# An early read of 32 bytes a row from the modulation weights, on Pool's queue, into a tile that nobody reads

## The chip, the cores and the metric

The kernel runs on one core of one Trainium2 chip. The metric is the device time of one execution in microseconds (us). The kernel before took 103.14 us, the median of three runs that went from 102.98 to 103.59.

## What is computed

The kernel is the attention half of a diffusion transformer block. With B = 2, N = 256 and D = 1152, all in bf16:

```python
mod = (_silu(c) @ w_mod).reshape(B, 6, 1, D)
shift_a, scale_a, gate_a, shift_m, scale_m, gate_m = [mod[:, i] for i in range(6)]
h = _layernorm(x, axis=-1) * (1 + scale_a) + shift_a
qkv = h @ wqkv
...
p = _softmax(jnp.einsum('bqd,bkd->bqk', q, k) * D ** (-0.5), axis=-1)
a = jnp.einsum('bqk,bkd->bqd', p, v) @ wo
return x + gate_a * a
```

The inputs are x (2 x 256 x 1152), c (2 x 1152), wqkv (1152 x 3456), wo (1152 x 1152) and w_mod (1152 x 6912). Of w_mod's six column groups three are needed: group 0 is the shift, group 1 the scale, group 2 the gate.

## The kernel before

The 512 rows of x are four tiles of 128 rows; D is nine blocks of 128. Every matrix product goes over these nine blocks. Five engines have lists of their own: PE (matrix products and transposes), DVE and ACT (elementwise work and copies out of the accumulators), POOL (setup, small powers, the gate's sum over partitions) and SP, which issues nearly all loads and stores. PE's, DVE's and ACT's orders are written out by hand: each operation is recorded in a list (all of these have line 75, that of the recording helper), and `pin` at the end chains each list. POOL's and SP's orders are left to a scheduler.

POOL begins with setup (L95 to L110): zeros in `ident` and, with `affine_select` (L97), ones on its diagonal; `ones_bf` (L102), `ones_row` (L104), `junk_rhs` (L106), `eps_t` (L108) and `neg_half` (L110). In the built program ones_bf is written ahead of the diagonal.

SP issues c (L115), two of x's four tiles (L118, ACT issues the other two), then w_mod's scale group in nine slices of 128 rows (L146), the first five 128-column blocks of wqkv (`wA`, L148 to L150), and the nine slices of the shift group (L153). Later come the rest of wqkv (L360), the gate group (L364) and wo (L368). Each transfer that SP or ACT issues takes one of eight completion semaphores in turn, and an issue waits until the transfer eight places before it has landed.

PE transposes c (needs c and ident), runs 13 junk matmuls on junk_rhs (N_JUNK), then starts the scale accumulators with ones_bf and ones_row and adds the nine scale blocks, one per slice, nine small matmuls each, with the transposes of the four normalized x tiles between them. DVE multiplies the transposed tiles by the scale (`hTs`); PE multiplies these by wA, with the nine shift blocks put between the later steps (H_AFTER_K). When the last shift block is done, h itself is formed (`hT`) and the rest runs: q and k, scores, v, softmax, attention, wo, gate.

The change and the steps of the prediction touch L94 to L110 (setup on POOL), L146 (`wm`, scale), L153 (`wm`, shift), the junk matmuls and `scale_block`. w_mod's slice kk is read as 128 rows of 2304 bytes; in the input a row is 13,824 bytes long. The first slice of the scale group is `w_mod[0:128, 1152:2304]`.

Of the kernel before, what the change touches and what calls it, by code (L numbers as in the profile page):

```python
# [11 lines left out]
BF16 = mybir.dt.bfloat16  # L12
# [4 lines left out]
def kernel(  # L17
# [9 lines left out]
    nc = tc.nc  # L27
    P = 128
    B, N, D = x.shape
# [23 lines left out]
    const = ctx.enter_context(tc.tile_pool(name="const", bufs=1))  # L53
# [32 lines left out]
    def pin(seq):  # L86
        names, insts = set(), []
        for r in seq:
            if r.ins.name not in names:
                names.add(r.ins.name)  # L90
                insts.append(r)
        for a, b in zip(insts, insts[1:]):
            tc.add_manual_dep(b.ins, a.ins.name, SCHED, reason="pinned engine order")

    ident = const.tile([P, P], BF16)  # L95
    nc.gpsimd.memset(ident, 0.0)
    nc.gpsimd.affine_select(  # L97
        out=ident, in_=ident, compare_op=ALU.not_equal, fill=1.0, base=0,
        pattern=[[-1, P]], channel_multiplier=1,
    )  # L100
    ones_bf = const.tile([P, P], BF16)
    nc.gpsimd.memset(ones_bf, 1.0)  # L102
    ones_row = const.tile([1, 512], BF16)
# [55 lines left out]
    for jj in range(N_JUNK):  # L159
# [7 lines left out]
        out=scT_f.rearrange("p k b -> p b k"),  # L167
# [117 lines left out]
    for k in range(KT):  # L285
        gi, jj = s_loc(k)
        for b in range(B):
            sl = slice(b * N, (b + 1) * N)
            vec.tensor_scalar(
                out=hTs[:, k, sl], in0=xnT[:, k, sl], scalar1=psS[gi][:, jj, b : b + 1], scalar2=None,  # L290
# [47 lines left out]
    for k in range(KT):  # L338
        for b in range(B):
            sl = slice(b * N, (b + 1) * N)  # L340
            if (2 * k + b) % 3 == 2:
                act_seq.append(sca.activation(
                    out=hT[:, k, sl], in_=xnT[:, k, sl], func=ACT.Identity,
                    bias=sh[:, k, b : b + 1], scale=s1p[:, k, b : b + 1],
                ))
            else:
                dve_seq.append(vec.tensor_scalar(
                    out=hT[:, k, sl], in0=xnT[:, k, sl],
# [23 lines left out]
    for f in range(NACC):  # L372
        for b in range(B):
            sl = slice(b * N, (b + 1) * N)
            if (f * B + b) % 2 == 0:
                dve_seq.append(vec.tensor_scalar(
                    out=qkT[:, f, sl], in0=accs[f][:, sl], scalar1=bias_sb[:, f, b : b + 1],
                    scalar2=None, op0=ALU.add))
            else:
                act_seq.append(sca.activation(  # L380
                    out=qkT[:, f, sl], in_=accs[f][:, sl], func=ACT.Identity,
# [18 lines left out]
    for b in range(B):  # L400
        vec.tensor_scalar(
            out=gacc[:, b, :], in0=wg_k[0], scalar1=scT_f[:, 0, b : b + 1], scalar2=None, op0=ALU.mult
        )
        for kt in range(1, KT):
            vec.scalar_tensor_tensor(
                out=gacc[:, b, :], in0=wg_k[kt],
# [37 lines left out]
    for b in range(B):  # L444
# [7 lines left out]
        for i in range(NQ):  # L452
            sca.activation(
                out=p_f[:, i, :], in_=s_ps[:, i, :], func=ACT.Exp,
# [111 lines left out]
```

## Time and profile before

| What | us |
|---|---|
| median of the runs | 103.14 |
| the profiled execution's span, first to last instruction | 101.7 |
| difference between the two, outside the span | 1.4 |
| PE busy in the span | 93.7 |
| DVE busy | 71.9 |
| ACT busy | 30.4 |
| POOL busy | 28.5 |
| DMA, 16 engines, mean rate over the span | 207 GB/s |
| a packet of 2304 bytes (a row of x or w_mod), median | 0.093 |
| a packet of 128 bytes, median | 0.013 |

The profiled execution's own time is its span; what the median holds beyond it lies before the first and after the last instruction. In the slices, the span is cut into 40 equal parts of 2.54 us, and a digit is the busy share in tenths. In the chain of waits each piece has a start, a length and what the time went to; DMA means that the next step waited for that transfer. In the list of waits the numbers are the total in us, how many times, and the longest. In the table by stretch each engine has its busy time and number of instructions, followed by the granted PE clock, the DMA engines' mean busy share and GB/s. In the list by time the columns are start, length, engine, line, operation, output and inputs, and in brackets how long the engine had been idle and what ended that.

### The profile page before, as it was taken

The page shows a single profiled execution, that of the slowest core. Times are in us where ns is not written, and L with a number is a line of the kernel's source. Part 1 is how long each engine was busy: PE and PEld are TensorE (multiplying, and loading weights), DVE is VectorE, ACT ScalarE, POOL GpSimd, SP SyncE. Part 2 cuts the span into 40 slices and gives each one's busy share as a digit, 9 for nine tenths or more (in the row PEclk, how much of TensorE's full clock was granted, in tenths as well). Part 3 has the DMA queues.
Part 4 walks back from the last instruction along what each step waited for, and adds up shares of the span by engine and source line. Part 5 has one row for each costly group of instructions (what it writes and reads, how often), then busy time and mean ns, then how long its engine had stood idle before and what let it go on. Part 6 is the DMA issues. An engine that isn't in the chain of part 4 may idle for free.

```text
span 101.7 us, 1828 instructions
## 1 busy us (share of the span) xinstructions
PE 93.7 (92%) x723; PEld 55.8 (55%) x729; DVE 71.9 (71%) x129; ACT 30.4 (30%) x61; POOL 28.5 (28%) x28
## 2 busy tenths in 40 slices
PE   0996989997999999999999999999998999999970
PEld 0334974474564444444447866566567856566550
DVE  0999679200899999999999992155226859998760
ACT  5089560000678422422332013551115500000000
POOL 6033300000000000079910000007990039996000
PEclk9999999999999999999999999999999999999999
DMA  2989999999999999999999100000000000202212
GB/s 75 376 304 396 403 391 386 405 395 325 354 374 361 400 377 322 316 327 327 368 406 366 50 0 0 0 0 0 0 0 0 6 0 0 116 0 116 114 54 67
DMA packets 17204, 21.05 MB, mean 207 GB/s; under 512 B 1068, under 2 KB 11692, under 8 KB 17196
## 3 DMA queue, kind: packets, MB, share of 16 engines
q1 hardware_dynamic: 16763, 20.34, 57.3%
q10 hardware_dynamic: 432, 0.61, 1.8%
q8 instruction: 5, 0.08, 0.3%
q14 instruction: 4, 0.02, 0.1%
HBM read 19.76 MB, written 1.18 MB: 206 GB/s over the span
## 4 chain that ended last, share of the span: by engine, by line
PE 71%; DMA 24%; issue 1%; DVE 0%; SPq 0%; ACT 0%
PE ps L75 63%; DMA wm<-in_w_mod_dram 21%; PE s_ps L75 4%; DMA x_sb<-in_x_dram 3%; PE acc_t L75 2%; PE bias_ps L75 1%; DVE pT L75 0%; PE psH L75 0%; SPq L115 0%; PE pT_ps L75 0%; ACT o_sb L75 0%
## 5 line engine op out<-in xcount | busy, mean ns | idle before, releaser
L409 POOL PARTITION_ALL_REDUCE gate_bc<-gacc x2 | 14.1, 7068 | 50.8 <-DVE gacc L75 32.9
L75 DVE SCALAR_TENSOR_TENSOR gacc<-wg_t,scT_f,gacc 128x1152 f32<-128x1152 bf16 x16 | 27.4, 1714 | 0.6
L75 PE MATMUL ps<-hT,wq_t 128*128 128x512 bf16 x114 | 25.3, 379 | 0.2
L75 PEld LDWEIGHTS <-wq_t 128*128 128x128 bf16 x117 | 11.3, 98 | 13.6
L75 PE MATMUL ps<-wq_t,hT 128*128 128x384 bf16 x108 | 17.7, 326 | 0.0
L75 PE MATMUL ps<-wo_t,attnT 128*128 128x384 bf16 x99 | 16.3, 326 | 0.0
L75 PEld LDWEIGHTS <-attnT 128*128 128x128 bf16 x117 | 10.9, 98 | 6.7
L75 PEld LDWEIGHTS <-hT 128*128 128x128 bf16 x108 | 10.6, 98 | 6.9
L75 ACT CAST qkT<-ps 128x512 bf16<-128x512 f32 x13 | 7.6, 585 | 15.4 <-PE ps L75 15.4
L483 POOL TENSOR_TENSOR wo_last<-wo_t,gate_bc 128x384 bf16<-128x384 bf16 x9 | 9.9, 1136 | 7.1 <-issue 7.1
L75 PE MATMUL acc_t<-hTs,wA 128*128 128x512 bf16 x42 | 9.9, 379 | 0.5 <-DVE hTs L75 0.4
L75 DVE TENSOR_TENSOR o_sb<-ga,x_sb 128x384 bf16<-128x384 f32 x11 | 8.1, 736 | 0.4
L75 PEld LDWEIGHTS <-wA 128*128 128x128 bf16 x90 | 5.4, 96 | 5.1 <-issue 0.5
L75 PEld LDWEIGHTS <-wm 128*128 128x128 bf16 x162 | 6.4, 97 | 3.1 <-DMA wm<-in_w_mod_dram 2.3
L75 ACT CAST v_sb<-ps 128x384 bf16<-128x384 f32 x8 | 3.8, 478 | 14.0 <-PE ps L75 14.0
L75 DVE TENSOR_TENSOR ga<-ps,gate_bc 128x384 f32<-128x384 f32 x11 | 6.1, 553 | 2.6 <-PE ps L75 2.5
L75 ACT ACTIVATE hT<-xnT,sh,s1p 128x256 bf16<-128x256 bf16 x6 | 3.1, 588 | 11.7 <-DVE sh L75 11.7
L75 PE MATMUL mps<-scT_rep,wm 128*128 128x96 bf16 x81 | 4.8, 207 | 0.8 <-DMA wm<-in_w_mod_dram 0.7
L75 DVE CAST sh_bf<-psH 128x18 bf16<-128x18 f32 x1 | 0.2, 176 | 7.4 <-PE psH L75 7.4
L75 ACT CAST o_sb<-ps 128x64 bf16<-128x64 f32 x1 | 0.2, 212 | 17.4 <-PE ps L75 17.4
L75 PE MATMUL junk_ps<-junk_rhs,ident 128*128 128x512 bf16 x13 | 4.6, 528 | 0.3 <-POOL neg_half L110 0.3
L75 DVE CAST v_sb<-ps 128x384 bf16<-128x384 f32 x4 | 2.1, 553 | 3.8 <-PE ps L75 3.8
(70 smaller groups left out, 81.3 us busy)
## 6 DMA issues: line engine op xcount, KB each, us to landing
wm<-in_w_mod_dram SPq DMA_DIRECT2D x18, 288.0 KB, 6.6
wq_t<-in_wqkv_dram SPq DMA_DIRECT2D x6, 864.0 KB, 9.7
wg_t<-in_w_mod_dram SPq DMA_DIRECT2D x9, 288.0 KB, 7.1
wo_t<-in_wo_dram SPq DMA_DIRECT2D x9, 288.0 KB, 6.2
wq_t<-in_wqkv_dram SPq DMA_DIRECT2D x2, 576.0 KB, 9.2
out_dram<-o_sb SPq DMA_DIRECT2D x3, 288.0 KB, 2.1
wA<-in_wqkv_dram SPq DMA_DIRECT2D x1, 800.0 KB
x_sb<-in_x_dram ACTq DMA_DIRECT2D x2, 288.0 KB, 3.5
```

Source lines behind the costliest of these rows:

```text
L75: r = fn(*a, **k)
L409: ar = nc.gpsimd.partition_all_reduce(gate_bc[:, b, :], gacc[:, b, :], P, bass.bass_isa.ReduceOp.add)
L483: nc.gpsimd.tensor_tensor(out=wo_last[:, k, :], in0=wo_k[k][:, D - TAILW :], in1=gate_bc[:, B - 1, D - TAILW :], op=ALU.mult)
```

## The change

After the diagonal is written, a tile of 128 rows by 16 columns (32 bytes a row) is read from the first 128 rows of w_mod, from column 1152 on, on POOL's queue. These are the first 32 bytes of each row of the first scale slice. A pin holds the transfer behind the `affine_select`. No instruction reads the tile.

```diff
-    nc.gpsimd.affine_select(
+    sel = nc.gpsimd.affine_select(
         out=ident, in_=ident, compare_op=ALU.not_equal, fill=1.0, base=0,
         pattern=[[-1, P]], channel_multiplier=1,
     )
+    touch = const.tile([P, 16], BF16)
+    touch_dma = nc.gpsimd.dma_start(out=touch, in_=w_mod[0:P, D : D + 16])
+    pin([sel, touch_dma])
```

In the built program POOL's order is then ident, ones_bf, the diagonal, the new transfer, ones_row, junk_rhs, eps_t, neg_half, and the rest as before. The order on PE, DVE, ACT and SP, and the semaphores that SP's and ACT's transfers take, are the same as before.

## Prediction

> **What bounds the kernel now.** I read the slices first, then the chain that ended last, then the waits up to 28 us, then the stretch from 1 to 10 us by microsecond and as a list. The slices give PE, DMA and the bytes moved:
>
> ```profile
> PE   0996989997999999999999999999998999999970
> DMA  2989999999999999999999100000000000202212
> GB/s 75 376 304 396 403 391 386 405 395 325 354 374 361 400 377 322 316 327 327 368 406 366 50 0 0 0 0 0 0 0 0 6 0 0 116 0 116 114 54 67
> ```
>
> PE is nearly full from the second slice, the DMA engines for 22 slices. Where both are full, the chain of waits says which one sets the end:
>
> ```profile
> ...
> 1.18 3.19 DMA x_sb<-in_x_dram
> ...
> 4.39 6.42 DMA wm<-in_w_mod_dram
> ...
> 10.83 8.72 DMA wm<-in_w_mod_dram
> ...
> 19.56 5.82 DMA wm<-in_w_mod_dram
> ...
> 25.43 0.41 PE psH L75 x9
> ```
>
> Up to 25.38 us the chain is transfers: x, then the scale and shift weights. After 25.43 it is PE with hardly a gap, to the last matmul at 98.45. So this change, which acts before 4 us, counts at the end only by what it does to the landing of the last shift weights (25.38), or by making PE so late that it is not ready there. The waits show how much room PE has:
>
> ```profile
> PE mps L75 <- DMA wm<-in_w_mod_dram: 0.7, 3, 0.3
> ...
> PE psH L75 <- DMA wm<-in_w_mod_dram: 0.4, 1, 0.4
> PE junk_ps L75 <- POOL neg_half L110: 0.3, 1, 0.3
> ```
>
> PE waited 0.7 + 0.4 = 1.1 us for w_mod rows: room for a late start, and the most that faster loading can win. The last line is the one place where PE waits for Pool's setup, which the change delays.
>
> **The change, part by part.**
>
> *Pool's issue.* One transfer is put on Pool's queue after the mask (L97) and before ones_row, junk_rhs, eps_t and neg_half. It waits for nothing. Call d the time for which Pool is held. No transfer on Pool's queue exists in this trace, so d is bounded. Below: the issues on SP, median 0.33 to 0.43 us. Above: 7.07 us, Pool's longest operation (the all-reduce; the unexplained idle time ahead of wo_last is as long, 7.1). Between: Pool is about twice as slow as VectorE at the same kind of work (tensor-tensor of 384 columns: 1136 ns on POOL, 553 on DVE), and twice an SP issue is 0.9 us. I take d = 0.9, nearer the low end, since it is one issue of 128 short rows. [...]
>
> Who is behind it: ACT needs eps_t at 8.26 and Pool's own rstd step needs neg_half at 6.59; both were ready at 2.66, so d up to 3.9 is hidden there. The mask is written before the transfer, so c's transpose is not touched. Left are the 13 junk matmuls and the ones matmuls, which start d later:
>
> ```profile
> 2.57 0.09 POOL L110 MEMSET neg_half<- 128x1 f32 x1
> 2.63 4.59 PE L75 MATMUL junk_ps<-junk_rhs,ident 128*128 128x512 bf16 x13 [0.29 <-POOL neg_half L110]
> 7.16 0.54 PE L75 MATMUL mps<-ones_row,ones_bf 1*128 1x96 bf16 x3
> 7.97 1.24 PE L75 MATMUL mps<-scT_rep,wm 128*128 128x96 bf16 x18 [0.28 <-DMA wm<-in_w_mod_dram]
> 10.14 0.56 PE L75 MATMUL mps<-scT_rep,wm 128*128 128x96 bf16 x9 [0.21 <-DMA wm<-in_w_mod_dram]
> ```
>
> PE is through with them at 7.16 + 0.54 = 7.70 and then eats a block of nine weight loads (0.41 us) whenever a slice lands, some 0.72 us apart. If it comes d later, blocks 0 to 2 run back to back and end at 7.70 + d + 3 x 0.41 = 8.93 + d. Block 3 cannot start before its rows land, at 10.14. So d up to 10.14 - 8.93 = 1.21 us costs nothing: cover is the transfer of the fourth slice. Above that, PE has 6.00 - 5.38 = 0.62 us idle between 20 and 26, again waits for shift weights; so cost begins at d of about 1.21 + 0.62 = 1.8, and is d - 1.8 from there. For d = 0.9: 0.
>
> One thing speaks against this. In the list of PE's weight loads, the junk loads start 0.43 us apart until 5.98 and then four within 0.74, so here the array became fast 3.35 us after the first junk matmul, although the granted clock reads 1.00 in every window. If the ramp moves with the start, nothing changes. [...] I keep the row, by which it is 0.
>
> *The transfer itself.* It is 128 rows of 32 bytes, eight for each of 16 DMA engines, into a queue of its own while x is being read. Below: 4 KB at 399 GB/s, 0.01 us. Above: c_sb, the nearest small read, was issued at 1.12 and had landed by 2.14; if an engine were held all that time, 1.02 us. Between: packets of 128 bytes take 13 ns each in the packet records, so eight cost 8 x 13 = 0.10 us, and the mark at the end 0.01. I take 0.11, nearest to a packet's own record. DMA engines are full there, so nothing hides it: it moves x and w_mod by 0.11 and the end with them. For x itself there is other cover: its last transposes start at 13.31 with their input ready at 11.92, 1.39 us.
>
> *What it can take away.* The loading is not even:
>
> ```profile
> 4.00:5.00 1.00, 1.00 (x4) 0.32 (x3) 0.97 (x3) 0.00 (x0) 0.00 (x0) 1.00 1.06 385
> 5.00:6.00 1.00, 1.00 (x4) 0.32 (x3) 0.97 (x3) 0.70 (x1) 0.00 (x0) 1.00 0.81 233
> 6.00:7.00 1.00, 1.00 (x6) 0.37 (x4) 1.00 (x4) 0.94 (x4) 0.67 (x2) 1.00 0.95 332
> 8.00:9.00 1.00, 0.88 (x17) 0.73 (x18) 1.00 (x3) 0.84 (x5) 0.72 (x2) 1.00 1.06 399
> ```
>
> The last column falls to 233 GB/s just as the first w_mod rows are due, and comes back. Against 399 the four microseconds from 4 to 8 (385, 233, 332 and 380) lose 14 + 166 + 67 + 19 = 266, or 0.67 us. If this is the price of reading w_mod for the first time, an earlier read of the very same rows could pay it. But there is no idle engine time to pay it in: x keeps them at 1.02 to 1.06 busy from 3 to 5 us, and a read issued after 1.65 + 0.9 = 2.55 is at the engines about 1 us ahead of those rows at best. Bounds: -1.1 (all of PE's waits for w_mod) to 0. I take 0: the stall is moved, not removed.
>
> Nothing else moves: the instruction order of PE, DVE, ACT and SP and the semaphores on which SP's issues wait stay as they are. Nobody reads the tile; it lands some 95 us before the end.
>
> Sum: 0 (Pool) + 0.11 (packets) + 0 (stall) = +0.11 on the span of 101.7. The median of 103.14 is 1.4 above that span; I leave those 1.4 alone: 103.14 + 0.11 = 103.25 us.
>
> **The rivals.**
>
> *A, slower: Pool is held long.* Place: L104 to L110 behind the new issue, then junk_ps. It decides from d = 1.8 us. [...] Against: every short Pool operation in this stage takes 0.09 to 0.67. At d = 3.3: +1.5 and the 0.11, 104.7; at 7.07, +5.3: 108.5.
>
> *B, slower: the small read holds the DMA engines.* If the slow first access is paid by the 32-byte rows and hidden by nothing, up to the 1.02 us above: 104.2. For: the engines are already over 1.0 busy there. Against: c's small packets did not hold x up visibly.
>
> *C, faster: the stall goes.* -0.67 gives 102.5; if the slowest engine lost more than the mean, up to -1.1: 102.0. For: the same rows are read, and the dip is the only one of this depth in the loads of 2304-byte rows up to 20 us. Against: the first weights of wqkv, another tensor, are read from 12 us without a dip (393 GB/s from 12 to 14), so "first access" is not shown to be the cause; and the lead is short.
>
> **How the numbers follow.** My case 0.34, A 0.24, B 0.18, C 0.24. One per cent is 1.03 us, about what a measurement of this kernel can tell from no change. Slower by more: 0.22 of A and 0.12 of B, 0.34. Faster by more: the part of C in which the slowest engine gains, 0.16. Within: 0.34 + 0.02 + 0.06 + 0.08 = 0.50. The range runs from C's far end, 102.0, to A at d = 3.2, 104.6; beyond lies the rest of A, about 0.12, and a little of C. My own case alone: 103.0 to 103.5.
>
> **What would show it.** Pool: the new issue's length is d, and junk_ps starts at 2.63 + d. If block 3 still starts within 0.2 of 10.14, Pool's delay was hidden. The rate from 5 to 7: still 233 and 332 says the stall stayed, 385 or more says C. The chain's last w_mod landing (25.38) is the verdict: 25.5 in my case, over 26.2 in B, under 24.8 in C. I am wrong if PE no longer waits for w_mod in the scale blocks (A), or if the time moves while the stretch up to 25.4 does not: then the cost lies around the span.

## The result, and the profile after

The changed kernel took 104.12 us, the median of seven runs (103.5 to 104.52), the kernel before 103.21 us in seven runs. The ratio is 1.0076 with a 95% interval of 1.0049 to 1.0103: 0.8% slower, within the stated range of 102.0 to 104.6 and within the 1% called "within", but outside the 103.0 to 103.5 that stood for the likeliest case alone. The profiled execution took 104.27 us with a span of 102.3.

First the same three rows of slices, of the changed kernel:

```profile
PE   0699989998899999999999999999998999999960
DMA  2999999999999999999999400000000000202211
GB/s 50 366 343 396 390 368 377 389 390 315 333 374 345 371 377 324 305 325 323 345 384 392 169 7 0 0 0 0 0 0 0 6 0 0 115 0 115 115 70 49
```

The fall in the third slice is less deep than before (343 against 304). But from the fifth slice on the rates are lower almost everywhere: 390 368 377 389 390 where 403 391 386 405 395 stood. The loads end later too: slice 23 moves 169 GB/s where it moved 50. That is far from the small read in time, and it is the first sign that the cause is not the read.

The chain that ended last (start, length, what):

```profile
...
1.20 3.73 DMA x_sb<-in_x_dram
...
4.95 5.49 DMA wm<-in_w_mod_dram
...
10.46 9.29 DMA wm<-in_w_mod_dram
...
19.76 6.06 DMA wm<-in_w_mod_dram
...
25.86 0.41 PE psH L75 x9
...
```

The chain has the same links as before. x lands 0.56 us later (4.93 against 4.37), yet the next link ends 0.37 earlier (10.44 against 10.81), and only after that is time lost: the third ends 0.2 late, the last 0.44 late (25.82 against 25.38). From there PE runs as before, and everything to the end is 0.44 later. The rest of the 0.6 us in this span lies in the last stores.

The waits of PE, and the start of the changed kernel by time:

```profile
PE junk_ps L75 <- POOL junk_rhs L109: 1.2, 1, 1.2
PE psH L75 <- DMA wm<-in_w_mod_dram: 0.9, 3, 0.4
```

```profile
1.61 0.86 POOL L102 DMA_DIRECT2D touch<-in_w_mod_dram  x1
...
3.51 5.11 PE L75 MATMUL junk_ps<-junk_rhs,ident 128*128 128x512 bf16 x13 [1.16 <-POOL junk_rhs L109]
...
9.03 1.71 PE L75 MATMUL mps<-scT_rep,wm 128*128 128x96 bf16 x36
...
10.57 0.67 PE L75 MATMUL tp<-ident,xn 128*128 128x128 bf16 x9
```

Pool is held for 0.86 us. PE's scale blocks begin 1.06 us later (9.03 against 7.97), then four blocks run back to back in one group of 36 instead of waiting for each slice, and the first transposes start at 10.57 against 10.54: the delay is gone by then. The wait for shift weights, 0.4 before, is 0.9 now: transfers are late, not PE.

The loading by microsecond:

```profile
4.00:5.00 1.00, 1.00 (x4) 0.34 (x3) 0.97 (x2) 0.00 (x0) 0.00 (x0) 1.00 1.05 410
5.00:6.00 1.00, 1.00 (x3) 0.29 (x2) 1.00 (x4) 0.40 (x1) 0.00 (x0) 1.00 0.96 301
6.00:7.00 1.00, 1.00 (x4) 0.41 (x3) 0.97 (x4) 0.97 (x3) 0.15 (x1) 1.00 1.01 362
```

The fall after 5 us is still there. It is shallower than before (301 and 362 against 233 and 332), but that is no sign of the change: in the second profile of the kernel before ("same", below) these two rates are 311 and 343, in the second of the changed kernel ("again") 169 and 236. Last, the queues (packets, MB, time of their packets as a share of 16 engines' span), of before and of after:

```profile
q1 hardware_dynamic: 16763, 20.34, 57.3%
```

```profile
q1 hardware_dynamic: 16763, 20.34, 58.6%
...
q0 software_dynamic: 32, 0.00, 0.1%
```

The new queue q0 costs 0.1% of the engines' time, about 0.1 us. But SP's queue needs more time for the very same 16763 packets: 57.3% of 101.7 is 58.3 us, 58.6% of 102.3 is 59.9. On average its packets became slower.

### The profile page after: what moved, and what is told of

Its sections match the earlier page's. It is cut to its first block, busy times and chain, and to the rows that moved or that the text cites. A ratio compares the mean times of both kernels' runs of the same rounds, so it can differ in the third digit from the quotient of the medians.

```text
span 102.3 us, 1830 instructions
## 1 busy us (share of the span) xinstructions
PE 93.7 (92%) x723; PEld 55.9 (55%) x729; DVE 72.4 (71%) x129; ACT 30.5 (30%) x61; POOL 29.6 (29%) x29
## 3 DMA queue, kind: packets, MB, share of 16 engines
q1 hardware_dynamic: 16763, 20.34, 58.6%
## 4 chain that ended last, share of the span: by engine, by line
PE 71%; DMA 24%; issue 1%; DVE 0%; SPq 0%; ACT 0%
PE ps L75 63%; DMA wm<-in_w_mod_dram 20%; PE s_ps L75 4%; DMA x_sb<-in_x_dram 4%; PE acc_t L75 2%; PE bias_ps L75 1%; DVE pT L75 0%; SPq L118 0%; PE psH L75 0%; PE pT_ps L75 0%; ACT o_sb L75 0%
## 5 line engine op out<-in xcount | busy, mean ns | idle before, releaser
L75 PE MATMUL junk_ps<-junk_rhs,ident 128*128 128x512 bf16 x13 | 5.1, 576 | 1.2 <-POOL junk_rhs L109 1.2
L75 PE MATMUL ps<-pT,v_sb 128*128 128x256 bf16 x36 | 4.1, 273 | 0.3 <-DVE pT L75 0.3
```

The source lines that it names most:

```text
L75: r = fn(*a, **k)
```

## The experiments

Theories, as they stood after the result: *hold* (Pool's 0.86 us costs), *transfer* (the small read slows the loads, or costs around the span), *first access* (the read pays, or moves, a price of w_mod's first rows), *chance*. The theory that survived, *address*, was formed after the second group of runs.

**The kernel before, against itself** (same). Nothing is changed.

> The kernel before, unchanged, against itself: ratio 1.000, the interval says what five rounds can tell. All theories agree. What it tells is how far the load rate and the landing of the last shift weights (25.38 us in the first profile of before) vary by themselves. Theory 'chance': rows of 2304 bytes vary by some 3 per cent between executions, so a mean near 99 ns and a landing near 25.8 can turn up here too. The other theories: mean packet of 2304 bytes near 97 ns and a landing within 0.15 of 25.38.

Ratio 1.0032, interval 1.0001 to 1.0062; last shift landing at 25.03, 385 GB/s from 10 to 25 us, 57.4% for q1. Two identical programs thus differ by 0.3%, and I claim nothing from less. The load rate after 10 us did not vary. The landing did, by 0.35, and that arises early: the link of the chain that ended at 10.81 in the kernel before ends at 10.32 here.

**The changed kernel again** (again). Nothing is changed.

> The changed kernel, unchanged, once more: ratio 1.005 to 1.010. Theory 'transfer' (the small read itself makes the loads slower or later, or costs outside the span): span 102.0 to 102.4, time minus span 1.9, last shift landing 25.7 to 25.9. Theory 'chance' for the loads: landing back near 25.4, and span near 101.8.

Ratio 1.0115 (1.0077 to 1.0153), a little above what was expected. The landing, 26.46, is later than any theory had it: in this profile the fall after 5 us is deeper (169 and 236 GB/s). The lower rate of the loads is back: 58.4% for q1, 340 GB/s from 25 to 50 us as in the changed kernel, against 351 before. "Chance" falls for the loads. Over all paired executions the time outside the span is 1.87 us here and 1.81 in the kernel before, so nothing of size is added around the span.

**The read behind Pool's setup** (late).

```diff
-    nc.gpsimd.memset(neg_half, -0.5)
+    neg = nc.gpsimd.memset(neg_half, -0.5)
+    touch = const.tile([P, 16], BF16)
+    touch_dma = nc.gpsimd.dma_start(out=touch, in_=w_mod[0:P, D : D + 16])
+    pin([neg, touch_dma])
```

> The small read stays on Pool's queue, but behind neg_half, so nothing in front of PE's junk matmuls is delayed. Theory 'hold' (Pool held for 0.86 us costs): junk_ps back at 2.63, ratio back to 1.000 to 1.003. Theory 'transfer': Pool's hold was hidden, so the ratio stays at 1.005 to 1.010 and the last shift landing at 25.7 to 25.9.

Ratio 1.008 (1.0052 to 1.0107); junk_ps back at 2.65, landing 26.22. Pool's hold is not the cause.

**Pool held, nothing read** (hold).

```diff
+    hold = const.tile([P, 512], BF16)
+    h1 = nc.gpsimd.memset(hold, 0.0)
+    h2 = nc.gpsimd.memset(hold[:, 0:384], 1.0)
+    pin([sel, h1, h2])
```

> No small read; in its place two writes of a tile that nobody reads hold Pool for some 0.85 us. Theory 'hold': ratio 1.005 to 1.010. Theory 'transfer': junk_ps starts near 3.5 as in the changed kernel, block 3 still near 10.14 us, ratio 0.998 to 1.002.

Ratio 0.9984 (0.9958 to 1.001). By time, the start of this kernel:

```profile
3.46 4.78 PE L75 MATMUL junk_ps<-junk_rhs,ident 128*128 128x512 bf16 x13 [1.12 <-POOL junk_rhs L110]
...
8.64 1.70 PE L75 MATMUL mps<-scT_rep,wm 128*128 128x96 bf16 x36
10.18 0.67 PE L75 MATMUL tp<-ident,xn 128*128 128x128 bf16 x9
```

PE is held as long as in the changed kernel, catches up with four blocks in a row, and nothing is lost. "Hold" falls.

**The read after all loads** (end), on Pool's queue behind the last product of wo_last; and **amid them** (mid), behind the third power.

```diff
-        nc.gpsimd.tensor_tensor(out=wo_last[:, k, :], in0=wo_k[k][:, D - TAILW :],
+        wl = nc.gpsimd.tensor_tensor(out=wo_last[:, k, :], in0=wo_k[k][:, D - TAILW :],
...
+    touch = const.tile([P, 16], BF16)
+    touch_dma = nc.gpsimd.dma_start(out=touch, in_=w_mod[0:P, D : D + 16])
+    pin([wl, touch_dma])
```

> The small read on Pool's queue behind Pool's last product (wo_last), when all loads have landed. Theory 'around' (a program with a transfer on Pool's queue costs a fixed time outside the span): time minus span 1.9 against 1.4, ratio 1.004 to 1.006, the loads as before. Theory 'loads' (the small read slows the loads beside and after it): ratio 0.999 to 1.002. Both together, as in the changed kernel, would be told apart by the span.

> The small read on Pool's queue behind the third power, near 11.5 us, amid the loads and when Pool is idle. Theory 'loads' (packets are slower after the small read): the last shift landing moves past 25.6 and the rows of 2304 bytes from 12 us on are slower; ratio 1.005 to 1.010. Theory 'early' (the harm is done at the first rows of w_mod): landing within 0.15 of 25.4, ratio below 1.004, except for what a fixed cost outside the span adds (0.5 us).

End: ratio 1.0057 (1.0032 to 1.0082), time outside the span 1.84. Mid: 1.007 (1.0037 to 1.0104). "Mid" gives the lower rate that "loads" expected (374 GB/s), but not its late landing (25.19). "End" misses what every theory said: "around" has the ratio right, with no time added around the span, and by both the loads should be as before. The read is issued at 93.1 us, and still the loads from 10 to 25 us run at 376 GB/s and q1 takes 58.8%. A transfer cannot slow what ended over 30 us before it. What these programs share with the changed one is not the transfer but the tile.

The change in "mid":

```diff
+    pows = []
...
-        nc.gpsimd.tensor_tensor(out=rstd[:, t : t + 1], in0=rstd[:, t : t + 1], in1=neg_half, op=ALU.pow)
+        pw = nc.gpsimd.tensor_tensor(out=rstd[:, t : t + 1], in0=rstd[:, t : t + 1], in1=neg_half, op=ALU.pow)
+        pows.append(pw)
...
     dve_norm(2)
+    touch = const.tile([P, 16], BF16)
+    touch_dma = nc.gpsimd.dma_start(out=touch, in_=w_mod[0:P, D : D + 16])
+    pin([pows[-1], touch_dma])
```

**The read on ACT's queue** (act), behind x, and **ahead of x** (act_first). The change in act_first; in act the same two lines stand behind the loop that issues x.

```diff
+    touch = const.tile([P, 16], BF16)
+    touch_dma = nc.scalar.dma_start(out=touch, in_=w_mod[0:P, D : D + 16])
     nc.sync.dma_start(out=c_sb, in_=c.rearrange("b (k p) -> (b k) p", p=P))
```

> The same small read on ACT's queue behind x's two tiles, none on Pool's. It takes one of the eight semaphores that SP and ACT share, which shifts the later transfers by one place. Theory 'queue' (it is Pool's queue that costs, not the read): ratio 0.998 to 1.002, time minus span 1.4. Theory 'read' (any read of these rows there costs): ratio 1.003 to 1.010.

> The same small read on ACT's queue ahead of x's two tiles, so that it is at the DMA engines near 1.8 us, well ahead of the first w_mod rows. Theory 'first access' (the fall to 233 GB/s from 5 to 6 us is the price of w_mod's first rows and can be paid early): the rate from 5 to 7 rises above 370, the last shift landing falls below 25.0, ratio 0.990 to 0.997. Theory 'not first access': the fall stays, ratio 1.000 to 1.006, since x comes 0.4 us later.

Act: 1.0055 (1.0022 to 1.0089), 377 GB/s; so it is not Pool's queue either. Act_first: 1.0107 (1.0059 to 1.0154), 374 GB/s from 10 to 25. Its small read landed 1.8 us after it was issued at 0.7, and this is the loading around it; first the kernel before, then act_first:

```profile
2.00:5.00 3.00, 2.56 (x7) 1.06 (x8) 2.28 (x6) 0.19 (x2) 0.66 (x4) 1.00 0.99 356
5.00:7.00 2.00, 2.00 (x8) 0.69 (x6) 1.97 (x6) 1.64 (x4) 0.67 (x2) 1.00 0.88 282
```

```profile
2.00:5.00 3.00, 2.56 (x7) 1.04 (x8) 2.00 (x5) 0.19 (x1) 0.65 (x4) 1.00 0.91 286
5.00:7.00 2.00, 2.00 (x6) 0.73 (x5) 1.97 (x6) 0.19 (x1) 0.39 (x2) 1.00 1.02 384
```

The fall from 5 to 7 is gone (384), and came back earlier: 286 from 2 to 5. The sum over 2 to 7 us is 3 x 356 + 2 x 282 = 1632 before and 3 x 286 + 2 x 384 = 1626 here, in KB. So the loss came earlier and was not removed. That the read moved it is not shown: ACT's two tiles of x are issued 0.4 to 0.5 us later here (1.17 and 1.67 against 0.75 and 1.16), which may have lowered the early rate too, and the sum varies by itself (3 x 350 + 2 x 327 = 1704 in "same").

**The theory "address".** In every program with the small read, wherever the read stands, its tile of 32 bytes a partition lies among the early ones, and each target of the loads of x, w_mod, wqkv and wo begins 32 bytes further than in the kernel before. In the built programs, w_mod's first slice lies at byte 182016 of each partition before (1422 x 128) and at 182048 after; x at 99968 (781 x 128) and 100000; wA at 37760 (295 x 128) and 37792. In the kernel before, these begin at multiples of 128. "Hold" had moved them by 1024, which keeps that, and was fast. In "end" the new tile is the last of its pool, so that the mask, the junk operand, c and the small tiles made from it keep their places; only the pools behind it move (weights, activations, temporaries), and the loads are as slow.

**Only a tile** (pad32): 32 bytes a partition, written once behind neg_half, nothing read; and **64 bytes** (pad64, with 32 columns in place of 16).

```diff
+    pad = const.tile([P, 16], BF16)
     ones_bf = const.tile([P, P], BF16)
...
-    nc.gpsimd.memset(neg_half, -0.5)
+    neg = nc.gpsimd.memset(neg_half, -0.5)
+    pin([neg, nc.gpsimd.memset(pad, 0.0)])
```

> The kernel before with a tile of 32 bytes a partition at the place where the small read's tile stands, written once by Pool behind neg_half; no extra transfer at all. Theory 'address' (the new tile moves every later tile by 32 bytes a partition, so that the loads' destinations no longer begin at multiples of 64): the loads are as slow as with the small read, that is, 370 to 380 GB/s from 10 to 25 us and rows of 2304 bytes at a median of 95 ns; ratio 1.004 to 1.009. Theory 'transfer' (the small read slows the loads): 385 GB/s, 93 ns, ratio 0.997 to 1.003.

> As pad32, with 64 bytes a partition. Theory 'address' with multiples of 64: 385 GB/s, 93 ns, ratio 0.997 to 1.003. If it is any move from the places of before that costs (or multiples of 128), it comes out like pad32: 370 to 380 GB/s, 95 ns, ratio 1.004 to 1.009. Theory 'transfer': as before, like pad32.

**The change with a tile of 512 bytes** (wide), of which 32 are read.

```diff
-    touch = const.tile([P, 16], BF16)
-    touch_dma = nc.gpsimd.dma_start(out=touch, in_=w_mod[0:P, D : D + 16])
+    touch = const.tile([P, 256], BF16)
+    touch_dma = nc.gpsimd.dma_start(out=touch[:, 0:16], in_=w_mod[0:P, D : D + 16])
```

> The changed kernel with the small read's tile made 512 bytes a partition, of which 32 are read as in the change; every later tile keeps its place modulo 512. Theory 'address': 385 GB/s from 10 to 25 us, 93 ns, ratio 0.998 to 1.003, although the read and Pool's hold of 0.86 us are those of the change. Theory 'transfer': 370 to 380 GB/s, 95 ns, ratio 1.005 to 1.010.

Two long stretches of the loads, last column GB/s, in the order before, after, pad32, pad64, wide:

```profile
10.00:25.00 15.00, 14.20 (x195) 9.78 (x197) 6.88 (x30) 3.17 (x5) 0.89 (x2) 1.00 1.06 385
25.00:50.00 25.00, 24.46 (x161) 11.92 (x163) 23.74 (x31) 10.84 (x21) 6.01 (x1) 1.00 1.08 351
```

```profile
10.00:25.00 15.00, 14.06 (x195) 9.69 (x193) 7.28 (x31) 3.47 (x5) 0.90 (x2) 1.00 1.07 375
25.00:50.00 25.00, 24.38 (x166) 12.05 (x170) 23.30 (x31) 10.85 (x21) 5.57 (x1) 1.00 1.09 340
```

```profile
10.00:25.00 15.00, 14.20 (x195) 9.54 (x192) 7.33 (x31) 3.25 (x5) 0.89 (x2) 1.00 1.07 375
25.00:50.00 25.00, 24.61 (x166) 11.90 (x163) 23.27 (x31) 10.85 (x21) 5.54 (x1) 1.00 1.09 341
```

```profile
10.00:25.00 15.00, 14.36 (x206) 10.00 (x204) 7.50 (x32) 3.07 (x5) 0.89 (x2) 1.00 1.07 376
25.00:50.00 25.00, 24.56 (x169) 12.03 (x170) 23.34 (x31) 10.85 (x21) 5.60 (x1) 1.00 1.10 341
```

```profile
10.00:25.00 15.00, 14.59 (x218) 10.33 (x215) 7.46 (x31) 3.21 (x5) 0.89 (x2) 1.00 1.05 385
25.00:50.00 25.00, 25.00 (x172) 12.17 (x169) 24.00 (x31) 10.85 (x21) 6.27 (x1) 1.00 1.09 350
```

A tile without any transfer gives the slow loads (375 and 341) and the loss: pad32 1.0086 (1.0056 to 1.0116), pad64 1.0076 (1.0039 to 1.0113). The change with its own transfer and its own hold, but with the tiles where they were modulo 512, gives the fast loads (385 and 350) and 1.0032 (0.9996 to 1.0067), as much as the kernel before against itself. "Transfer" falls, "address" stands. Its guess of multiples of 64 was wrong: a move by 64 costs as much as one by 32.

**Ahead of x, with the wide tile** (act_first_wide): act_first with the tile and the slice of "wide", the candidate for a version better than both.

> The small read on ACT's queue ahead of x, with the tile made 512 bytes a partition. Theory 'address' with a first access that can be paid early: rate from 5 to 7 above 370, last shift landing below 24.9, ratio 0.993 to 0.998, faster than both kernels. Theory 'address' with a first access that is only moved (what act_first gained from 5 to 7 us it had lost from 2 to 5): last shift landing 25.0 to 25.4, ratio 0.999 to 1.005. Theory 'transfer': as act_first, ratio 1.007 to 1.013.

Ratio 1.0034 (1.0002 to 1.0066), landing 25.16, 384 GB/s from 10 to 25. An early read gains nothing here either, and no version beat the kernel before.

All runs together, sorted by where the tiles lie:

| Run | Tiles moved by | GB/s 10-25 | GB/s 25-50 | q1 share | last shift landing, us | ratio |
|---|---|---|---|---|---|---|
| before | 0 | 385 | 351 | 57.3% | 25.38 | |
| same | 0 | 385 | 351 | 57.4% | 25.03 | 1.0032 |
| hold | 1024 | 384 | 351 | 57.8% | 24.77 | 0.9984 |
| wide | 512 | 385 | 350 | 57.4% | 25.12 | 1.0032 |
| act_first_wide | 512 | 384 | 349 | 57.5% | 25.16 | 1.0034 |
| after | 32 | 375 | 340 | 58.6% | 25.82 | 1.0076 |
| again | 32 | 379 | 340 | 58.4% | 26.46 | 1.0115 |
| late | 32 | 372 | 340 | 58.8% | 26.22 | 1.008 |
| end | 32 | 376 | 341 | 58.8% | 25.41 | 1.0057 |
| mid | 32 | 374 | 341 | 59.2% | 25.19 | 1.007 |
| act | 32 | 377 | 340 | 58.8% | 25.98 | 1.0055 |
| act_first | 32 | 374 | 340 | 58.9% | 25.66 | 1.0107 |
| pad32 | 32 | 375 | 341 | 59.0% | 25.44 | 1.0086 |
| pad64 | 64 | 376 | 341 | 59.0% | 25.78 | 1.0076 |

No row of the one group has a rate of the other. Single landings overlap (25.19 in "mid", 25.38 in the kernel before), but the mean landing is 25.09 in the first five and 25.77 in the other nine: 0.68 us. That is the size of the loss, since the mean ratios of the two groups, 1.002 and 1.008, lie 0.6% or 0.62 us apart. Behind the landing nothing differs: the span less the landing is 76.4 to 76.7 us in all fourteen profiles.

The rate accounts for a part of the 0.68. From 10 to 25 us, 10 GB/s less is 150 KB, or 0.40 us at 375 GB/s. The landings agree: from that of the last scale slice to that of the last shift slice the five took 11.67 us on average (11.47 to 11.86), the nine 12.08 (11.84 to 12.38), 0.41 more. The other 0.27 arose ahead of the last scale slice, which lands at 13.25 to 14.29 us in the nine and at 13.30 to 13.70 in the five. The fall after 5 us differs there from profile to profile, and no run shows that this part belongs to the places of the tiles.

## Why the prediction was right or wrong

- *What bounds the kernel* was right: the loss passes through the landing of the last shift weights, and behind it PE is as before. The sign I named for it was too fine: 25.5 for my case against 25.38, where two profiles of the same program lie 0.35 apart. The 25.82 measured lies between my case and B's 26.2.
- *Pool's issue*: d = 0.9 was taken, 0.86 measured, and the cover named (the fourth slice's landing) held: 10.57 against 10.54 in the changed kernel, and "hold" lost nothing. The sign I named for rival A, that PE no longer waits for w_mod in the scale blocks, did appear, without A: PE was late there and in time again at the first transposes. It was a bad sign to name.
- *The clock*: I kept the row "fast 3.35 us after the first junk matmul". It was one draw. The 13 junk matmuls took 4.30 to 5.73 us in these profiles; with the same start of 2.63 they took 4.59, 5.13 and 5.66 (before, act, act_first). The trace also has a record of the clock that I did not use: its first entry, a full clock, begins at 5.38 to 9.14 us in the fourteen profiles. In the nine where the junk matmuls quicken on the way, from 0.43 to 0.22 us apart, they do so within 0.2 us of that entry (5.98 and 5.96 in the kernel before). So "1.00 in every window" was no reading ahead of it. No run shows what sets the place of that entry, which differs by 3.76 us between the fourteen. A long stretch of junk matmuls is mostly hidden, as d is: the chain passes through them in one profile of the fourteen. That is "wide", where the long case (5.70) met Pool's hold and PE did become the path; its chain begins so:

```profile
1.65 0.82 POOL touch L102
...
3.51 5.70 PE junk_ps L75 x13
9.21 2.11 PE mps L75 x39
```

- *The transfer*: 0.11 us of engine time was forecast, and q0's 0.1% of the span is 0.10; the packet records add up to 0.13 us an engine. The working was not right all the same. The read went as 16 packets of 256 bytes, as many as there are engines, and 16 marks of 4 bytes, not as eight packets an engine, and its packets took 15 to 551 ns each. The same sum is 0.41 us in "again" and 0.03 in "mid". So 0.11 was near by luck, and no run shows a loss of time by the transfer itself.
- *The stall*: taking 0 for it was right, but the change itself did not put "moved, not removed" to the test. I gave the read a lead of some 1 us; it had none. It landed 4.9 us after its issue, at 6.5, in the middle of the fall. In act_first it had the lead, and the fall came earlier, but x's later issue there may have done that.
- *What failed* is "Nothing else moves: the instruction order of PE, DVE, ACT and SP and the semaphores on which SP's issues wait stay as they are". That is true of orders and semaphores, and the addresses moved by 32 bytes. The missing term is the loads' 2.7% from 10 to 25 us, some 0.40 us. With it the sum is 0.11 + 0.40 = 0.51 on 103.21, or 103.72, against a measured 104.12. The 0.40 that is left is little more than the 0.33 us by which two identical programs differed, and its cause stays open.
- *1.4 us around the span* paired a median with the span of another execution. Executions with their own spans give 1.81 us for the kernel before and 1.87 for the changed one. It does not touch the difference.

So "0.8% slower" was inside the range, but by luck: its cause was in none of the rivals, since neither A nor B had the tile itself in it.

## What to carry to other kernels

A tile that nobody reads was not free here (0.9% in pad32, 0.8% in pad64): in a pool that places tiles one behind another it moves all later ones. Before adding a small tile, note where the load targets begin; give it a size that keeps them there (512 bytes a partition did here, 32 and 64 did not), and judge an experiment that adds a tile only beside one that adds the tile alone. When the same packets of the same queue take longer from one program to the next, as here (57.3% and 58.6% of the span), look at addresses as well as at queues.

## What the runs showed of the hardware

- A move of the tiles by 32 or 64 bytes a partition cost 2.6% of the load rate from 10 to 25 us (385 to 375 GB/s; 372 to 379 in the nine profiles); moves by 512 and 1024 cost none (384 to 385). Moves by 128 and 256 were not tried, so if a multiple decides, no run tells 128, 256 and 512 apart. In the packet records, from 18 to 20 us, 1% of the 2304-byte packets of before took 94 to 130 ns instead of 93, and 81% of after; the 4-byte marks at the end of a transfer took more than 9 ns in none and in 64%.
- It does not begin with the loads. From 6 to 10 us, with the same moved targets, 2 to 3% of the 2304-byte packets of after took 94 to 130 ns, and 1 to 2% of before; from 10 to 12 us it is 23% against none, from 16 to 18 it is 83% against 17%. So a moved target alone is not enough. That it comes from PE and DVE at work on moved tiles beside the transfers was not shown: from 7 to 10 us, ahead of it, they were busy for 3.00 and 2.92 of the 3 us. Whether the loads' own tiles or those of the activations have to be moved, no run told apart. The mechanism stays open.
- Where in its partition a target begins did not by itself set the time of its rows: in the kernel before, x at byte 99968 and w_mod at 182016 both took a median of 93 ns a row of 2304 bytes, and so did w_mod at 182048 in the changed kernel from 6 to 10 us.
- A read of 4 KB on Pool's queue held Pool for 0.86 us in the change and landed 2.2 us after its issue when the DMA engines were 0.2 to 0.3 busy ("end", issued at 93.1), but 4.9 to 6.3 us after it beside the loads ("mid", 6.1, held Pool for 0.98).
